# Expert 7's weights in a permanent place and loaded first, both static blocks in rounded halves within the last queries, half of the weights loaded there

## The chip, the cores and the metric

The kernel runs on one core of a Trainium2 chip. The metric is device time in microseconds (us) of one execution, lower is better. Engines: TensorE (PE; PEld is its weight load), VectorE (DVE), ScalarE (ACT), GpSimd (POOL) and SyncE (SP, which here issues loads and does index arithmetic). SBUF is the on-chip memory, PSUM the small memory that TensorE writes into.

## What is computed

Agent attention, and on its output a routed mixture of experts. B = 4 batches, N = 11456 rows, C = 128; 49 agents; 8 experts with F = 1024.

```
a2k = softmax(agents @ k.T);  agent_v = a2k @ v
x   = softmax(q @ agents.T) @ agent_v              # 45824 rows in all
use = x @ w_skip > 0                               # the others are returned as they are
e   = argmax(x @ w_gate);  g = softmax(x @ w_gate)[e]
out = x + g * (relu(x @ w1[e]) @ w2[e])            # for the rows in use
```

## The kernel before

**Attention** (`attention`, lines 167 to 944). Each batch is cut into 15 chunks of 6 columns of 128 rows, 60 chunks in all. One loop over 79 slots writes out the instructions of all engines in a fixed order (`manual_schedule`): within a slot the words of `ORDER[phase]` (lines 46 to 51) are gone through, and each engine executes its own instructions in the order in which they were written. A slot's number below is counted from the first query slot, as in the variable `at`. Keys, values and queries of different batches overlap ("w"); from slot 46 on only queries of batch 3 are left ("q"). There a slot n does, in this order:

- "qN": `query_norm` of chunk n-4 on VectorE (L479 reciprocal, L487 twice), which frees the only `ps_x` buffer; "qD": `query_weight`, every second slot (L526, L527 on VectorE, L530 on POOL)
- "sQ": `scores` of chunk n-1 on TensorE (L355); "qS": its maximum on VectorE (L444); "qE": six exponentials on ACT (L450)
- "qG": the gate's maximum on VectorE (L516), subtraction on POOL (L517), exponential on ACT (L518), every second slot
- "qT": transposes on TensorE (L458) and a copy on ACT (L460); "qO": the output DMA, on ACT's queue
- "rt", "rx": a step of the router (`codes`, `ranks`, `routing`; mostly VectorE, some POOL)
- "mX": `query_mix` of chunk n-3 on TensorE (L471), which needs `ps_x`; "sb", "sa": `static` before and after it
- "wt": one conversion of weights, if due (below)

**Loads.** `prefetch` (lines 820 to 835) goes through a list of loads in the order of the slots that need them, up to eight slots ahead, and stops where no buffer is free. There are 13 buffers (`many`): 8 tiles `ld` (`few`) and 5 in the region `lds`. SP issues the loads, each after the last reader of its buffer.

**Weights.** An expert's weights come in four tiles of 256 KB. `weights` (line 332) rounds a tile to the high half on ACT (L340, fp32r) and subtracts on POOL for the low half (L341). Experts 0 to 5 have a permanent place, `w`, and start every 1.95 slots from slot 2 on. Expert 7's halves lie in `late`, over the ring of scores, and start at slots 47 to 50; expert 6's lie in `shared`, over `lds`, at slots 61 to 64. Expert 7's float32 tiles stay in their buffers (`st["whole"]`) for the static blocks.

**Static blocks.** The first two blocks of 384 rows of expert 7 are known once batch 0 is routed. They are computed within attention, in float32: `layer1` (line 746, L749), ReLU on ACT (L750), `layer2` (line 752, L756), two steps behind. `STATIC` says how many items of the list are done by which slot: block 0 in slots 50 to 60, block 1 from slot 61 on into the last `routing`, which calls `static` four times. `sums` (L761) copies a block's sum on ACT. `early_rows` brings the rows, and `early_x` (line 787: L790 on ACT, L791 on VectorE, at slot 64) the rows of the first dynamic block.

**Dynamic blocks** (`experts`, lines 947 to 1409). 37 blocks of 384 rows, one expert after the other, 7 first. `block` (line 1374) does 48 products of rounded operands (three per tile: high x high, low x high, high x low; L1363, L1369), transposes (L1357, L1351) and the index products (L1344); the low half of the hidden layer is L1190 on VectorE. Expert 7 has a loop of its own (lines 1402 to 1404); `passed` (line 986) then branches (L989) to the code of the others, with a hint that `block` put into TensorE's stream (`mark_branch_hint_location`). Its own code is aligned at its end (line 992).

## Time and profile before

| what | us |
|---|---|
| median of three runs | 709.5 |
| lowest, highest | 707.9, 710.36 |
| the profiled execution | 710.59 |
| its span, first to last instruction | 708.8 |

The page gives busy time over the span: TensorE 633.8 us (89%), its weight load 583.6, VectorE 519.8, ACT 370.0, POOL 359.6. Of the span's slices the DMA row is at 8 or 9 tenths for the first 15 of 40 (about 266 us) and at 1 in the second half. Matmul ends are modelled, so a busy TensorE is not one at its peak. In the timeline each row has start, length, engine, line, operation, output<-input, count, and in brackets how long the engine had been idle before it and what ended that. A float32 product is two records (x2), a rounded one is one.

### The profile page before, as it was taken

To read this page: it belongs to the slowest core of one execution; us is meant where nothing else is said; L and a number is where in the kernel's file an instruction comes from. 1 tells how busy PE (TensorE), PEld (TensorE's weight loads), DVE (VectorE), ACT (ScalarE), POOL (GpSimd) and SP (SyncE) were. 2 spreads that over 40 slices of the span, in tenths; PEclk is the share of its full clock that TensorE was granted. 3 is DMA by queue.
4 is the path that set the end of the run, shared out by engine and by line. 5 is a ranking of instruction groups with operands and counts; after the bars stand their busy time and mean duration, and the time that the engine had idled before them with its cause. 6 is when DMAs were issued, how large, how long until landed. Compare 5 with 4: busy or idle time off the path is not lost. (4 is left out here: it accounts for less than half of the span.)

```text
span 708.8 us, 20720 instructions
## 1 busy us (share of the span) xinstructions
PE 633.8 (89%) x6776; PEld 583.6 (82%) x6776; DVE 519.8 (73%) x1797; ACT 370.0 (52%) x1036; POOL 359.6 (51%) x457
## 2 busy tenths in 40 slices
PE   5689789878897879995799799999999999999995
PEld 5589678767786767673589799999999999999995
DVE  4226657887878777766678588888888888888784
ACT  3346466546454655554255355555555555555552
POOL 2322352256335463303476456666666666666653
PEclk9799899989978995999799899999999999999998
DMA  8999899999999896443022111111111111111100
GB/s 315 356 365 324 284 365 397 385 337 349 396 353 332 283 359 236 159 153 140 24 56 50 38 31 41 41 45 41 45 41 45 45 45 41 42 43 46 42 30 9
DMA packets 59677, 119.20 MB, mean 168 GB/s; under 512 B 14982, under 2 KB 23306, under 8 KB 59600
## 3 DMA queue, kind: packets, MB, share of 16 engines
q1 hardware_dynamic: 43184, 79.92, 32.5%
q10 hardware_dynamic: 8928, 23.79, 8.5%
q0 software_dynamic: 7488, 14.54, 7.2%
q8 instruction: 40, 0.66, 0.4%
q14 instruction: 37, 0.30, 0.1%
HBM read 87.18 MB, written 31.50 MB: 167 GB/s over the span
## 5 line engine op out<-in xcount | busy, mean ns | idle before, releaser
L1255 ACT ACTIVATE hh<-h 128x384 fp32r<-128x384 f32 x296 | 145.1, 491 | 98.2 <-ACTq L974 94.0
L1190 DVE SCALAR_TENSOR_TENSOR hl<-h,hh 128x384 fp32r<-128x384 f32 x296 | 155.9, 553 | 35.2 <-DVEq L974 31.4
L1281 POOL DMA_INDIRECT xg<-out_dram,ids x108 | 110.0, 1018 | 84.7 <-issue 74.3
L1295 POOL DMA_INDIRECT out_dram<-xo,sid x117 | 116.9, 999 | 46.0 <-issue 33.8
L1369 PE MATMUL y<-hh,w 128*128 128x384 f32 x512 | 136.7, 348 | 0.1
L1363 PE MATMUL h<-xh,w 128*128 128x384 f32 x512 | 132.4, 340 | 3.9 <-PEq L974 3.9
L450 ACT ACTIVATE qe<-ps_s,qm 128x49 f32<-128x49 f32 x360 | 75.4, 313 | 42.3 <-DVE qm L444 35.0
L1363 PEld LDWEIGHTS h<-xh,w 128*128 128x128 f32 x512 | 93.8, 190 | 4.5 <-issue 4.5
L1369 PEld LDWEIGHTS y<-hh,w 128*128 128x128 f32 x512 | 89.1, 189 | 0.2 <-issue 0.2
L1363 PE MATMUL h<-xl,w 128*128 128x384 f32 x256 | 87.1, 340 | 0.0
L1369 PE MATMUL y<-hl,w 128*128 128x384 f32 x256 | 86.3, 337 | 0.0
L355 PE MATMUL ps_s<-agT,ld 128*64 128x49 f32 x1728 | 67.2, 237 | 15.2 <-DMA ld<-in_k_dram 6.2
L355 PEld LDWEIGHTS ps_s<-agT,ld 128*64 128x64 f32 x1728 | 62.6, 152 | 20.8 <-issue 12.2
L471 PE MATMUL ps_x<-av,eT 50*128 50x138 f32 x720 | 65.1, 318 | 2.4 <-DVE G L487 2.3
L471 PEld LDWEIGHTS ps_x<-av,eT 50*128 50x128 f32 x720 | 51.9, 206 | 14.1 <-issue 10.5
L487 DVE TENSOR_TENSOR xs<-ps_x,qr 128x768 f32<-128x768 f32 x60 | 57.5, 959 | 5.6 <-DMA out_dram<-xs 2.2
L444 DVE TENSOR_REDUCE qm<-ps_s 128x6 f32<-128x294 f32 x60 | 27.4, 457 | 40.4 <-PE ps_s L355 38.3
L395 POOL TENSOR_TENSOR scores<-scores,mb 128x294 f32<-128x294 f32 x60 | 44.7, 771 | 24.0 <-DVE mb L390 24.0
L355 PEld LDWEIGHTS ps_s<-agT,lds 128*64 128x64 f32 x1152 | 41.7, 150 | 10.0 <-issue 3.2
L355 PE MATMUL ps_s<-agT,lds 128*64 128x49 f32 x1152 | 45.7, 236 | 3.8 <-ACT qe L450 2.0
L1363 PEld LDWEIGHTS h<-xl,w 128*128 128x128 f32 x256 | 48.8, 190 | 0.0
L1251 ACT ACTIVATE yT<-y 128x384 f32<-128x384 f32 x37 | 18.1, 490 | 58.6 <-ACTq L974 58.6
(199 smaller groups left out, 1078.8 us busy)
## 6 DMA issues: line engine op xcount, KB each, us to landing
out_dram<-xs ACTq DMA_DIRECT2D x60, 387.0 KB, 6.4
ld<-in_v_dram SPq DMA_DIRECT2D x37, 387.0 KB, 6.7
ld<-in_k_dram SPq DMA_DIRECT2D x37, 384.0 KB, 7.0
ld<-in_q_dram SPq DMA_DIRECT2D x35, 384.0 KB, 6.3
lds<-in_q_dram SPq DMA_DIRECT2D x25, 384.0 KB, 6.0
lds<-in_v_dram SPq DMA_DIRECT2D x23, 387.0 KB, 7.5
lds<-in_k_dram SPq DMA_DIRECT2D x23, 384.0 KB, 7.5
ld<-in_moe_w_dram SPq DMA_DIRECT2D x23, 256.0 KB, 5.8
```

Of the source, the lines that this page charges most:

```text
L355: r.append(ten.matmul(pt[h : h + 64, t * NA : (t + 1) * NA], lhsT=xT[:, t * P + h : t * P + h + 64], rhs=agT[:, b, :], start=True, stop=True))
L395: pool.tensor_tensor(out=x, in0=x, in1=st["mb", chunks[n][0]].unsqueeze(1).to_broadcast(x.shape), op=ALU.subtract)
L444: vec.tensor_reduce(st["qm", n], st["qs", n], axis=AX.X, op=ALU.max, negate=True)
L450: act.activation(qes[n % PAR["qe"]][:, t, :NA], s[:, t, :], AF.Exp, bias=mx[:, t : t + 1])
L471: ten.matmul(px[:, h, t, :], lhsT=eT[s, t * P : (t + 1) * P], rhs=st["av", b][s, :], start=True, stop=True)
L487: vec.tensor_tensor(out=out[:r, h, j, :], in0=px[:r, h, j, w], op=ALU.mult, in1=rs[:r, h, j].unsqueeze(3).to_broadcast(list(px[:r, h, j, w ...
L1190: v.scalar_tensor_tensor(out=hl[:, f], in0=h_ps[f % HB], scalar=0.0, in1=hh[:, f], op0=ALU.max, op1=ALU.subtract).then_inc(sem["HL"], 1)
L1255: s.activation(hh[:, f], h_ps[f % HB], AF.Relu).then_inc(sem["HH"], 1)
L1281: g.indirect_dma_start(out=xg[n % TURN][:, h, :], out_offset=None, in_=out, in_offset=bass.IndirectOffsetOnAxis(ap=ids[:, n % TURN, h : h ...
L1295: g.indirect_dma_start(out=out, out_offset=bass.IndirectOffsetOnAxis(ap=sid[:, n % 2, h : h + 1], axis=0), in_=xo[:, n % 2, h, :], in_offs ...
L1363: w = t.matmul(h_ps[f % HB], lhsT=ps.w1[e][wx][:, cs], rhs=x, start=(n == 0), stop=(n == 2))
L1369: w = t.matmul(y_ps, lhsT=ps.w2[e][wx][:, f, :], rhs=h[:, f], start=(f == 0 and n == 0), stop=(f == FC - 1 and n == 2))
```

## The change

1. Places: the list of places is reordered, so that expert 5 gets `shared`, expert 6 `late`, and expert 7 the sixth part of `w`.
2. Order of the weights: 7, 0, 1, 2 every 2.7 slots from slot 2 to 42; 3, 4, 5, 6 every 0.9 slots from slot 46 to 59. No float32 tile stays behind.
3. Buffers: 5 `ld`, 3 `more`, 5 `lds`. From slot 41 on loads take `ld` only. The hidden halves of the static blocks, `hs`, lie over `more`.
4. Static blocks: three rounded products for each float32 one. `layer1` writes the high half on ACT and the low half on VectorE; `layer2` reads both. `rows` makes a high half on ACT and a low half on VectorE of the rows of blocks 0 and 1 and of the first dynamic block. All 38 items stand in slots 48 to 61, after "mX"; `routing` calls `static` no more.
5. `key_shift` of batch 0 (L395): every second chunk on VectorE in place of POOL.
6. The loop of expert 7's blocks is aligned to 256 instructions on TensorE.

```diff
-PAR = dict(cols=6, ld=8, more=5, qe=3, eT=2, xs=5, tail=3, first=3, ahead=2, h=4,
-           weights=(12, 195, 100), late=(-13, 1))
-STATIC = {("sa", i - 10): 2 + i * 16 // 10 for i in range(11)}
-STATIC.update({("sb", 1): 18, ("sb", 2): 20, ("sa", 2): 25})
+PAR = dict(cols=6, ld=5, more=5, qe=3, eT=2, xs=5, tail=3, first=3, ahead=2, h=3, few=-6,
+           weights=((2, 270), (46, 90)))
+STATIC = {("sa", i): 38 + (i - 1) * 37 // 13 for i in range(-12, 2)}
...
-        parts += [[x[:, i * F : (i + 1) * F] for i in range(4)] for x in (self.shared, late)]
+        parts[-1:-1] = [[x[:, i * F : (i + 1) * F] for i in range(4)] for x in (self.shared, late)]
...
+        size = PAR["h"] * PAR["cols"] * (C + 1)
+        self.more = a("more", [P, -(-size // 32) * 32], F32).ap()[:, :size]
+        self.hs = nc.alloc_sbuf_tensor_at("hs", [P, PAR["h"], 2, TB], F32R, offset=nc.sbuf_base - -(-size // 32) * 128).ap()
...
-        many = few + [ps.lds[:, i * LD : (i + 1) * LD] for i in range(PAR["more"])]
+        rooms = [ps.more[:, i * LD : (i + 1) * LD] for i in range(PAR["h"])]
+        many = few + rooms + [ps.lds[:, i * LD : (i + 1) * LD] for i in range(PAR["more"])]
...
-            pool.tensor_tensor(out=x, in0=x, in1=st["mb", chunks[n][0]].unsqueeze(1).to_broadcast(x.shape),
+            eng = vec if n < NCH and n % 2 else pool
+            eng.tensor_tensor(out=x, in0=x, in1=st["mb", chunks[n][0]].unsqueeze(1).to_broadcast(x.shape),
...
-                static(28)
...
-                static(31)
...
-                static(len(items))
...
+        def rows(x):
+            pt = turned_rows((x - 1) % TURN)
+            behind(act.copy(ps.xh, pt), st["last"])
+            behind(vec.tensor_tensor(out=ps.xl, in0=pt, in1=ps.xh, op=ALU.subtract), st["last"])
+            if x == AHEAD_STATIC:
+                behind(pool.tensor_copy(ps.db, ps.drow[:, 0, :].unsqueeze(1).to_broadcast([P, 2 * NB, sh.NC + 1])), st["last"])
...
+        def layer1(f):
+            pt = ps_s.tile([P, 512], F32, name="ps_s")[:, :TB]
+            for n, (w, x) in enumerate(((0, ps.xh), (1, ps.xh), (0, ps.xl))):
+                ten.matmul(pt, lhsT=ps.w1[NE - 1][w][:, f * P : (f + 1) * P], rhs=x, start=(n == 0), stop=(n == 2))
+            i = f % PAR["h"]
...
+            hi, lo = (ps.hs[:, i, x, :] for x in range(2))
+            before = reads.get(id(rooms[i]), [])
+            behind(act.activation(hi, pt, AF.Relu), before)
+            behind(vec.scalar_tensor_tensor(out=lo, in0=pt, scalar=0.0, in1=hi, op0=ALU.max, op1=ALU.subtract), before)
...
+        def layer2(f):
             if f == 0:
+                st["y"] = ps_a.tile([P, 512], F32, name="ps_a")[:, :TB]
+            for n, (w, h) in enumerate(((0, 0), (1, 0), (0, 1))):
+                ten.matmul(st["y"], lhsT=ps.w2[NE - 1][w][:, f, :], rhs=ps.hs[:, f % PAR["h"], h, :],
+                           start=(f == 0 and n == 0), stop=(f == FC - 1 and n == 2))
...
         for x in range(2):
+            items.append((rows, x))
+            for f in range(FC + PAR["ahead"]):
+                items += [(layer1, f)] * (f < FC) + [(layer2, f - PAR["ahead"])] * (f >= PAR["ahead"])
             items.append((sums, x))
             if x == 0:
                 items.append((first_result,))
+            else:
+                items.insert(-1, (rows, AHEAD_STATIC))
...
-        early_w = [(e, i) for e in range(NE - LATE) for i in range(4)]
...
+        for (at, step_), es in zip(PAR["weights"], ((NE - 1, 0, 1, 2), (3, 4, 5, 6))):
+            for j, n in enumerate((e, i) for e in es for i in range(4)):
+                starts.setdefault(sh.Q0 + at + j * step_ // 100, []).append(n)
...
-                bufs = few if kind == "w" and n[0] >= NE - LATE else many
+                bufs = many if i < late + PAR["few"] else few
...
-                if at == n_all + 4:
-                    early_x()
...
+            t.addr_align(256, offset=0, max_nops=0)
             with t.While(ps.left[0]):
                 hint = block(NE - 1, t.mark_branch_hint_location)
```

## Rows read from the trace of the kernel before

**Rows 1.** Busy time by stretch: stretch length, engines' busy us, granted clock, DMA share, GB/s.
```profile
30.00:40.00 10.00, 10.00 (x140) 9.91 (x140) 0.00 (x0) 6.28 (x14) 9.29 (x13) 0.75 0.88 289
100.00:200.00 100.00, 85.95 (x1597) 75.49 (x1595) 76.61 (x239) 54.47 (x204) 39.52 (x67) 0.93 1.01 375
260.00:284.00 24.00, 21.74 (x185) 17.19 (x184) 17.81 (x64) 13.78 (x52) 9.44 (x15) 0.58 0.75 261
284.00:322.00 38.00, 35.47 (x444) 25.16 (x444) 27.48 (x79) 22.45 (x87) 7.53 (x20) 1.00 0.44 151
```

**Rows 2.** Timeline, POOL, the key shifts of batch 0.
```profile
28.49 10.80 POOL L395 TENSOR_TENSOR scores<-scores,mb 128x294 f32<-128x294 f32 x15 [24.00 <-DVE mb L390]
```

**Rows 3.** Lines L374 and L1190: ns least/median/most, first and last start.
```profile
L374 DVE TENSOR_TENSOR run<-scores,run x56: 400/466/1139, 9.5 to 220.3; 128x294 f32<-128x294 f32 x56
...
L1190 DVE SCALAR_TENSOR_TENSOR hl<-h,hh x296: 543/554/559, 350.5 to 698.6; 128x384 fp32r<-128x384 f32 x148
```

**Rows 4.** DMA issues, KB each, median us to landing: 275 to 300 us, then all.
```profile
lds<-in_q_dram SPq DMA_DIRECT2D x3, 384.0 KB, 3.1
...
ld<-in_v_dram SPq DMA_DIRECT2D x37, 387.0 KB, 6.7
```

**Rows 5.** Timeline, PE, two products of the static block 1.
```profile
329.17 0.81 PE L756 MATMUL ps_a<-ld,ld 128*128 128x384 f32 x2
329.81 0.81 PE L749 MATMUL ps_s<-run,ld 128*128 128x384 f32 x2
```

**Rows 6.** Timeline, one query slot with a static product, 303.9 to 307.4 us.
```profile
303.98 0.46 DVE L444 TENSOR_REDUCE qm<-ps_s 128x6 f32<-128x294 f32 x1 [0.96 <-PE ps_s L355]
304.34 0.98 PE L471 MATMUL ps_x<-av,eT 50*128 50x138 f32 x12
...
304.48 1.26 ACT L450 ACTIVATE qe<-ps_s,qm 128x49 f32<-128x49 f32 x6 [1.50 <-DVE qm L444]
...
305.37 0.20 DVE L479 RECIPROCAL qr<-ps_x 128x6 f32<-128x6 f32 x1
...
305.77 0.51 ACT L460 COPY eT<-ps_e 128x384 f32<-128x384 f32 x1
...
306.20 0.49 ACT L750 ACTIVATE ld<-ps_s 128x384 f32<-128x384 f32 x1
...
306.53 0.20 DVE L487 TENSOR_TENSOR G<-ps_x,qr 128x54 f32<-128x54 f32 x1
...
306.94 0.23 DVE L527 RECIPROCAL gs<-gs 128x12 f32<-128x12 f32 x1
```

**Rows 7.** Timeline, DVE, L479 of slots 48 and 61 (of 60, one per chunk).
```profile
269.11 0.20 DVE L479 RECIPROCAL qr<-ps_x 128x6 f32<-128x6 f32 x1 [0.30 <-PE ps_x L471]
...
319.23 0.20 DVE L479 RECIPROCAL qr<-ps_x 128x6 f32<-128x6 f32 x1 [0.76 <-PE ps_x L471]
```

**Rows 8.** Timeline, the end of attention.
```profile
328.68 0.14 DVE L516 TENSOR_REDUCE top<-G 128x6 f32<-128x48 f32 x1
...
330.17 1.26 POOL L341 TENSOR_TENSOR shared<-ld,shared 128x512 fp32r<-128x512 f32 x1 [4.76 <-ACT shared L340]
...
333.84 0.56 DVE L791 TENSOR_TENSOR xl<-ps_s,xh 128x384 fp32r<-128x384 f32 x1 [4.26 <-ACT xh L790]
...
343.87 0.16 DVE L670 SCALAR_TENSOR_TENSOR rec<-ps_e,every 128x8 f32<-128x8 f32 x1
345.58 0.48 ACT L761 COPY yT<-ps_a 128x384 f32<-128x384 f32 x1 [2.09 <-PE ps_a L756]
```

**Rows 9.** Line L989, the branches behind expert 7, of SP's and TensorE's queues: ns.
```profile
L989 SPq COMPARE_BRANCH  x1: 45/45/45, 365.9 to 365.9; - x1
L989 PEldq COMPARE_BRANCH  x1: 3184/3184/3184, 397.6 to 397.6; - x1
```

**Rows 10.** Timeline, PE, the transpose L1357 of four blocks, one per block.
```profile
390.40 0.49 PE L1357 MATMUL yt<-ident,yT 128*128 128x128 f32 x3
...
405.21 0.41 PE L1357 MATMUL yt<-ident,yT 128*128 128x128 f32 x1
...
415.35 0.49 PE L1357 MATMUL yt<-ident,yT 128*128 128x128 f32 x3
...
424.57 0.27 PE L1357 MATMUL yt<-ident,yT 128*128 128x128 f32 x1
```

## The prediction

> **What bounds the kernel now.** I read the stretches first [rows 1]. From 100 to 200 us the DMA engines are busy all the time (share 1.01) and TensorE is not. [...] From 284 to 322, the last queries, DMA is at 0.44 and the clock is full: no bandwidth limit there, but a chain of short operations per slot. Behind that comes the router's chain on VectorE [rows 8], and then the blocks, on TensorE without gaps but for one, behind expert 7 [rows 9, 10]. So a saving counts if it is DMA traffic before 260 us, a link of the slot chain in the last queries, a link of the router's chain, or that gap. The profiled execution took 710.59 us, 1.8 more than its span and 1.1 over the median of 709.5; the sum is made on 710.59, and 1.1 is taken off at the end.

> **Key shifts of batch 0 (L395).** Fifteen run on POOL back to back, 10.80 us, 0.72 each [rows 2]. Seven go to VectorE, where the nearest form (L374, same tile) takes 0.47 at the median and up to 1.14 [rows 3]. If both engines worked freely, the eight left would end 5.0 us earlier. What that can return is the DMA time lost meanwhile: share 0.88 over 30 to 40 us against 1.01 later [rows 1], 1.3 us. I take -0.5, as L374's spread shows that it is held up at times; ends 0 and -1.3. [...]

> **Weights later.** Counting the starts by hand, 23 tiles of 256 KB are due before query slot 45 now and 16 then: 7 fewer. At 375 GB/s [rows 1] one takes 0.70 us, 7 take 4.9. That holds while DMA is full, and by 260 us it is no longer. I take -3.0; ends 0 and -4.9. The tiles moved to slots 46 to 59 meet a DMA share of 0.44: nothing there.

> **Five load buffers from slot 41 on.** Walking the load loop by hand, in these slots every load is now issued two or more slots ahead of its use. After the change value chunks 56 and 58 take a buffer that the scores of queries 42 and 43 free one slot earlier, and TensorE has only a mix (L471, 0.98 us [rows 6]), a transpose and one value chunk in between, about 2 us. A load lands in 3.1 us in a quiet stretch and in 6.7 at the median [rows 4]. Each of the two waits is then 1 to 4.7 us. I take +2.5 for both, near the quiet end; ends 0 and +9.

> **The static blocks in halves.** On TensorE they get cheaper: a float32 product (two records) starts 0.64 us after the one before it [rows 5], 32 of them take 20.5 us. The steady loop does 48 rounded products and nine small ones in 9.22 us [rows 10], at most 0.19 each; 96 take 18.2. That is not the bound. The bound is the order on VectorE. After the change each first-layer step issues two evictions: the high half on ACT, then the low half on VectorE, which needs the high half. Both stand at the end of a slot (after "mX", as "sa"). So on VectorE the low half stands **ahead of the next slot's L479**, and on ACT the high half stands behind that slot's six exponentials (L450) and copy (L460), which need L444, which is behind L479. That closes a ring through both engines that is open now, since the ReLU feeds only TensorE. [Rows 6] show one slot: L479 starts at 305.37 although the ReLU (L750) ends only at 306.69. With the low half ahead of it, L479 would start at 306.69 + 0.1 + 0.55 = 307.34, 2.0 us later; 0.55 is L1190, the same operation [rows 3]. One crossing of this kind exists now: L791 kept VectorE idle for 4.26 us until ACT came to L790 [rows 8].

> The ring: from L479 to the end of L527 1.80, but only to the end of L487, 1.36, in every second slot: 1.6; from L444 to the end of the ReLU 306.69 - 303.98 = 2.7; a hand-over and the low half 0.65. Together 4.95 us a slot. By the new STATIC table VectorE gets 18 such writes in 12 slots (48 to 53 and 55 to 60; slot 54 has none). 12 x 4.95 = 59.4; six writes beyond the first of a slot, 0.55 each, 3.3; slot 54 as now, 3.5; the lead that VectorE has over ACT is lost once, 2.0; the first result in slot 55, a transpose and a copy, 1.0. Sum 69.2 us from the L479 of slot 48 to that of slot 61. Now these 13 slots take 319.23 - 269.11 = 50.1 [rows 7]. So +19.1; slot 61, with the third split of rows, adds about 1. **I take +20.** [...]

> The eight more conversions in these slots (POOL 1.26 each [rows 8], half of that on ACT) fall into the idle part of the ring; without the ring ACT, now busy 22.45 of 38 us [rows 1], still has room for 5 more.

> **The end of attention.** Expert 6's conversions leave the router's chain. Now POOL works on L341 until 331.43, and VectorE waits for L791 and goes on with the router at 334.40, although L516, on which the next step rests, was done at 328.82 [rows 8]. Without the conversions that step needs two short operations on POOL and ACT, about 1.2 us. That is -4.3, and the chain to L670 behind it stays. L670 ends at 344.03, but ACT's copy of the second static block at 346.06 [rows 8], and only then can the blocks begin; the copy moves to slot 61, another -2.0. I take -6.3; ends -2 and -7.

> **Aligned loop of expert 7.** The branch behind it (L989) took TensorE's queue 3184 ns, SP's branch of the same line 45 ns [rows 9]; both have a hint ahead. From transpose to transpose that block took 405.21 - 390.40 = 14.81 us and the next 10.14, against 9.22 in the steady loop [rows 10]: 6.5 us in all. If the branch becomes like SP's, -6.0, with half a microsecond left over; if not, 0. I take -6.0, at three in four. [...]

> **Sum.** -0.5 - 3.0 + 2.5 + 20 - 6.3 - 6.0 = +6.7: 717.3 on the profiled execution, **716.2 us** on the median.

> **The rivals.**
> 1. *The branch still misses* (the alignment doesn't do what it is there for). For: the hint is there now and fails. Against: SP's 45 ns. 716.2 + 6.0 = 722.2.
> 2. *Faster: VectorE's idle time swallows the low halves.* Place: the last queries, where VectorE is busy 27.48 of 38 us [rows 1]; 18 x 0.55 = 9.9 us fit into the 10.5 idle. [...] It decides where the 13 slots grow by less than 1.0 us each, since the other terms sum to -13.3. For: the shares. Against: the order of the queues, as told, and L791's 4.26 us.
> 3. *The loads starve.* With five buffers the two waits cost 9 and not 2.5: 722.7. For: the landings of 6.7 us under load. Against: DMA is at 0.75 by then.

> **How the numbers follow.** Forecast 0.46 (its own range 710 to 721), rival 1 0.17, rival 2 0.27, rival 3 0.10. About 0.3%, 2.1 us, can be told from no change: 707.4 to 711.6 is the same. Rival 2 lies below 707.4 in most of its range (0.24) and the forecast in little of its own (0.01): faster 0.25. Same: 0.03 of rival 2 and 0.10 of the forecast. The rest, 0.62, is slower. From 700 to 723 lie 0.45 of the forecast and 0.13, 0.17 and 0.06 of the rivals: 0.81.

> **What would show it.** In the changed profile L479 should come every 5 us in slots 49 to 61, with ACT's high half as what ended VectorE's idle time before the new low half, and TensorE should wait at L471 for L487. L989 on TensorE's queue should be under 0.4 us, and the block behind it near 9.3. From the end of the last L516 to the end of L670 it should be 11 us, now 15.2. I am wrong if the slots stay under 4.5 us, if the branch takes 3 us again, or if the value chunks of slots 44 and 45 wait more than 3 us each.

## The result, and the profile after

The changed kernel takes 709.95 us, the kernel before in the same rounds 707.13 (medians of 20 runs each): ratio 1.0063 [1.0038, 1.0088], slower by 4.4 us by the ratio (the medians alone differ by 2.8). The fourth set below gave 1.0070 [1.0038, 1.0103]. Slower was forecast (+6.7 us), 716.2 was not: the kernel before came out 2.4 us under the 709.5 on which the sum stood, and the change at two thirds of its size.

In the second and third of the four sets of runs below every traced kernel's blocks took some 12.3 us instead of 9.2, and a run, of the kernel before too, about 820 us (the third set's chip gave 705 later), so that their ratios are compared within a set, and their traces read for the branch and for what comes ahead of the blocks.

Five starts carry the comparison. L479 starts once per slot (chunk n in slot n + 4), so that its starts in slots 4, 44, 48 and 61 (chunks 0, 40, 44 and 57 in the expectations) cut attention in three; then come the last L479 and the first block. All from the timeline, in us:

| kernel | first L479 | slots 4 to 44 | 44 to 48 | 48 to 61 | run against before |
|---|---|---|---|---|---|
| before | 56.94 | 194.17 | 18.00 | 50.12 | |
| changed | 56.81 | 185.18 | 23.20 | 67.61 | 1.0063 |
| changed, fourth set | 56.25 | 187.84 | 23.44 | 70.06 | 1.0070 |

The stretches of the changed kernel, which answer to [rows 1] (length, busy us of TensorE, its weight loads, VectorE, ACT, POOL; granted clock, DMA share, GB/s; the last queries now end at 341 us):
```profile
30.00:40.00 10.00, 10.00 (x143) 9.94 (x142) 4.33 (x5) 5.17 (x14) 5.71 (x7) 0.77 0.87 294
100.00:200.00 100.00, 87.07 (x1689) 77.06 (x1690) 79.39 (x248) 56.29 (x215) 38.92 (x69) 0.95 1.00 372
260.00:284.00 24.00, 18.97 (x209) 15.69 (x209) 17.91 (x62) 13.90 (x48) 10.97 (x13) 0.79 0.68 224
284.00:337.00 53.00, 41.67 (x473) 35.22 (x473) 33.00 (x94) 30.41 (x103) 19.49 (x30) 0.97 0.56 184
```
In the last queries no engine is full: TensorE, the busiest, works 41.67 of 53 us, VectorE 33.00. What VectorE waits for in that stretch, and what TensorE waits for (us in total, times, longest):
```profile
DVE hs L751 <- ACT hs L750: 14.3, 11, 2.6
...
PE ps_x L471 <- DVE G L487: 11.9, 10, 2.0
```
L751 is the new low half, L750 the high half. One slot of the changed kernel, as [rows 6] show one of before:
```profile
307.52 0.45 DVE L444 TENSOR_REDUCE qm<-ps_s 128x6 f32<-128x294 f32 x1
...
307.75 1.75 PE L471 MATMUL ps_x<-av,eT 50*128 50x138 f32 x12 [1.95 <-DVE G L487]
...
308.01 1.26 ACT L450 ACTIVATE qe<-ps_s,qm 128x49 f32<-128x49 f32 x6 [1.23 <-DVE qm L444]
...
309.43 1.01 PE L745 MATMUL ps_s<-xh,w 128*128 128x384 f32 x2
...
310.79 0.49 ACT L750 ACTIVATE hs<-ps_s 128x384 fp32r<-128x384 f32 x1 [0.85 <-PE ps_s L745]
...
311.31 0.56 DVE L751 SCALAR_TENSOR_TENSOR hs<-ps_s,hs 128x384 fp32r<-128x384 f32 x1 [1.88 <-ACT hs L750]
...
312.08 1.08 DVE L751 SCALAR_TENSOR_TENSOR hs<-ps_s,hs 128x384 fp32r<-128x384 f32 x2 [0.21 <-ACT hs L750]
...
313.09 0.18 DVE L479 RECIPROCAL qr<-ps_x 128x6 f32<-128x6 f32 x1
...
314.59 0.97 PE L471 MATMUL ps_x<-av,eT 50*128 50x138 f32 x12 [1.22 <-DVE G L487]
```
The circle (the prediction's ring) can be read off it: the mix (L471), behind it TensorE's static product (L745), ACT's high half, 1.88 us of idle VectorE, the low half, and only then the L479 and L487 for which TensorE's next mix has waited 1.22 us.

What answers to [rows 8]: the router's last steps, then TensorE's first block.
```profile
342.87 0.14 DVE L516 TENSOR_REDUCE top<-G 128x6 f32<-128x48 f32 x1
...
352.76 0.16 DVE L667 SCALAR_TENSOR_TENSOR rec<-ps_e,every 128x8 f32<-128x8 f32 x1
...
355.14 0.98 PE L1347 MATMUL h<-xh,w 128*128 128x384 f32 x2 [2.67 <-PEq L958]
```
The branch behind expert 7, of [rows 9], is now L973 (ns), and the transposes of [rows 10] are L1341:
```profile
L973 SPq COMPARE_BRANCH  x1: 45/45/45, 373.1 to 373.1; - x1
L973 PEldq COMPARE_BRANCH  x1: 370/370/370, 404.7 to 404.7; - x1
```
```profile
397.65 0.49 PE L1341 MATMUL yt<-ident,yT 128*128 128x128 f32 x3
...
407.61 0.49 PE L1341 MATMUL yt<-ident,yT 128*128 128x128 f32 x3
```
The block with the branch takes 9.96 us (14.81 before), the next 9.20.

### The profile page after: what moved, and what is told of

Same layout as the page of the kernel before. It is cut to its first block, busy times and chain, and to the rows that moved or that the text cites. A ratio compares the mean times of both kernels' runs of the same rounds, so it can differ in the third digit from the quotient of the medians.

```text
span 709.9 us, 20810 instructions
## 1 busy us (share of the span) xinstructions
PE 621.0 (87%) x6808; PEld 582.7 (82%) x6808; DVE 529.5 (75%) x1822; ACT 368.8 (52%) x1036; POOL 356.4 (50%) x450
## 5 line engine op out<-in xcount | busy, mean ns | idle before, releaser
L1353 PE MATMUL y<-hh,w 128*128 128x384 f32 x592 | 157.1, 346 | 1.3 <-PEq L958 1.2
L1347 PE MATMUL h<-xh,w 128*128 128x384 f32 x592 | 153.2, 340 | 3.6 <-PEq L958 3.5
L1347 PEld LDWEIGHTS h<-xh,w 128*128 128x128 f32 x592 | 107.4, 190 | 8.8 <-issue 8.7
L1353 PEld LDWEIGHTS y<-hh,w 128*128 128x128 f32 x592 | 102.5, 188 | 1.6 <-issue 1.6
L450 ACT ACTIVATE qe<-ps_s,qm 128x49 f32<-128x49 f32 x360 | 75.4, 311 | 52.6 <-DVE qm L444 45.4
L1347 PE MATMUL h<-xl,w 128*128 128x384 f32 x296 | 100.6, 340 | 0.0
L1353 PE MATMUL y<-hl,w 128*128 128x384 f32 x296 | 99.0, 335 | 0.0
L471 PE MATMUL ps_x<-av,eT 50*128 50x138 f32 x720 | 64.2, 314 | 19.0 <-DVE G L487 18.3
L471 PEld LDWEIGHTS ps_x<-av,eT 50*128 50x128 f32 x720 | 51.7, 203 | 30.7 <-issue 23.9
L354 PE MATMUL ps_s<-agT,ld 128*64 128x49 f32 x1320 | 53.3, 238 | 11.7 <-DMA ld<-in_k_dram 6.1
L354 PEld LDWEIGHTS ps_s<-agT,ld 128*64 128x64 f32 x1320 | 49.1, 153 | 17.2 <-issue 13.2
L487 DVE TENSOR_TENSOR xs<-ps_x,qr 128x768 f32<-128x768 f32 x60 | 57.5, 959 | 3.9 <-DVE qr L479 0.5
L1353 PEld LDWEIGHTS y<-hl,w 128*128 128x128 f32 x296 | 55.6, 188 | 0.0
L395 POOL TENSOR_TENSOR scores<-scores,mb 128x294 f32<-128x294 f32 x53 | 41.1, 801 | 23.8 <-DVE mb L389 23.8
L444 DVE TENSOR_REDUCE qm<-ps_s 128x6 f32<-128x294 f32 x60 | 26.8, 446 | 32.1 <-PE ps_s L354 30.0
L1235 ACT ACTIVATE yT<-y 128x384 f32<-128x384 f32 x37 | 18.2, 491 | 58.1 <-ACTq L958 58.1
L354 PE MATMUL ps_s<-agT,lds 128*64 128x49 f32 x1008 | 37.5, 228 | 5.9 <-ACT qe L450 4.7
```

The lines of the kernel that those rows point to most:

```text
L354: r.append(ten.matmul(pt[h : h + 64, t * NA : (t + 1) * NA], lhsT=xT[:, t * P + h : t * P + h + 64], rhs=agT[:, b, :], start=True, stop=True))
L395: eng.tensor_tensor(out=x, in0=x, in1=st["mb", chunks[n][0]].unsqueeze(1).to_broadcast(x.shape), op=ALU.subtract)
L444: vec.tensor_reduce(st["qm", n], st["qs", n], axis=AX.X, op=ALU.max, negate=True)
L450: act.activation(qes[n % PAR["qe"]][:, t, :NA], s[:, t, :], AF.Exp, bias=mx[:, t : t + 1])
L471: ten.matmul(px[:, h, t, :], lhsT=eT[s, t * P : (t + 1) * P], rhs=st["av", b][s, :], start=True, stop=True)
L487: vec.tensor_tensor(out=out[:r, h, j, :], in0=px[:r, h, j, w], op=ALU.mult, in1=rs[:r, h, j].unsqueeze(3).to_broadcast(list(px[:r, h, j, w ...
```

## The experiments

**1. Without the directive** (first set, as 2 to 4).
```diff
-            t.addr_align(256, offset=0, max_nops=0)
```

> The changed kernel without the one alignment directive ahead of expert 7's loop; everything else is the change. Theory (the directive alone cures the first return of the loop): TensorE's branch goes from 370 ns back to about 3.2 us, the block behind it from 9.96 us back to some 14.8, and the run is 5 to 6.7 us slower than the changed kernel, about 1.5% above the kernel before. Rival A (the shorter loop cured itself, because the static blocks moved elsewhere and the code lies otherwise now): the branch stays under 0.5 us and the time does not move. Rival B (the branch comes back but the blocks of SyncE or POOL wait anyway): branch 3 us, the time 0 to 2 us slower.

Ratio 1.0069 [1.0033, 1.0105], as with it, and the branch keeps its 369 ns:
```profile
L973 PEldq COMPARE_BRANCH  x1: 369/369/369, 408.5 to 408.5; - x1
```
The theory fell, rival A held. In the changed kernel the directive does nothing that the runs can tell; something else had cured the branch.

**2. The low halves one slot later.** L751 is put on a list and issued in the next slot behind "qN qD", ahead of "sQ".
```diff
-    "q": "qN+4 qD+5 sQ+1 qS+1 ...
+    "q": "qN+4 qD+5 lo sQ+1 qS+1 ...
```

> The changed kernel with one thing moved: VectorE's low half of a static layer is issued one query slot later, right after that slot's first query work, instead of right behind the high half of its own slot; the same instructions, the same number of them. Theory (the ring: within a slot VectorE waits in order for ACT's high half, ACT for TensorE's product, TensorE for what VectorE gives): the slots from chunk 44 to 57 go from 5.2 us (67.6 us for 13) back to 3.9 to 4.2, and the run is 12 to 15 us faster than the changed kernel, some 697 us. Rival A (VectorE is simply loaded: the low halves and the key shifts fill it): the same work in another order gives under 3 us. Rival B (the loads cannot follow at 3.9 us a slot, so the wait passes to the value and query loads): about half, 5 to 8 us, and waits on DMA appear in the slots from 50 on.

Ratio 0.9893 [0.9853, 0.9933], 699.34 us: 1.7 points below the changed kernel, 12 us. Slots 48 to 61 take 53.90 us in place of 67.61, with the same instructions. The waits in the last queries, 284 to 326 us:
```profile
ACT qe L450 <- DVE qm L444: 6.2, 9, 1.2
...
PE ps_s L354 <- DMA ld<-in_q_dram: 1.8, 1, 1.8
```
The two waits of the circle are down to 0.3 us (L471 on L487) and 0.9 us (the low half, now L779, on ACT), where the changed kernel had 11.9 and 14.3. Over the same 268 to 322 us in both kernels they are
```profile
PE ps_x L471 <- DVE G L487: 2.3, 2, 1.9
...
DVE hs L779 <- ACT hs L750: 0.9, 3, 0.4
```
against 8.8 and 13.3 us in the changed kernel. The order on VectorE is shown to be the cause: a cause in its load would have stayed, since the instructions are the same. Some 3.8 us over the 50.12 of the kernel before are left.

**3. More load buffers until three slots later.**
```diff
-PAR = dict(..., few=-6,
+PAR = dict(..., few=-3,
```

> The changed kernel with the three buffers of the later hidden halves given to loads until three slots later (few=-3 for -6); nothing else. Theory (the value chunks of slots 41 to 43 came late because only five buffers were left when they were issued, which cost 5.2 us between chunk 40 and 44): TensorE's two waits on value loads of 1.98 and 1.02 us go, the stretch from chunk 40 to 44 shrinks by about 5 us, and the run is 4 to 5 us faster. Rival (the ring sets the end of the queries whatever comes earlier, or the loads are bound by the traffic of expert weights and not by buffers): the stretch does not shrink, or what it gains is lost by chunk 57; under 1 us.

Ratio 1.0013 [0.9983, 1.0042], 3.5 us under the changed kernel (4 to 5 expected). Slots 44 to 48 take 19.61 us (23.20), the other two stretches 187.72 and 67.90. In the changed kernel these two waits stood at the value chunks, and here none:
```profile
250.91 0.87 PE L412 MATMUL ps_a<-ld,scores 128*49 128x129 f32 x12 [1.98 <-DMA ld<-in_v_dram]
...
252.80 1.26 PE L412 MATMUL ps_a<-ld,scores 128*49 128x129 f32 x12 [1.02 <-DMA ld<-in_v_dram]
```
The ring did not swallow the gain, nor give any.

**4. The kernel before with the directive.**
```diff
+            t.addr_align(256, offset=0, max_nops=0)
             with t.While(ps.left[0]):
```

> The kernel before with only the alignment directive ahead of expert 7's loop. Theory: the first return costs TensorE 0.37 us instead of 3.18 and the block behind it 9.96 us instead of 14.8; the run is 5 to 6.7 us faster than before, ratio near 0.991. Rival (the code's place before the loop decides, and in the kernel before 256-byte alignment is not what was missing): no change within 0.3%.

Ratio 0.9927 [0.9890, 0.9963], 5.2 us faster. The branch takes 370 ns, the block 10.04 us, the next 9.24:
```profile
386.30 0.49 PE L1357 MATMUL yt<-ident,yT 128*128 128x128 f32 x3
...
396.34 0.49 PE L1357 MATMUL yt<-ident,yT 128*128 128x128 f32 x3
...
405.58 0.49 PE L1357 MATMUL yt<-ident,yT 128*128 128x128 f32 x3
```
So there the directive is worth all of the term, and in the changed kernel nothing (1). Attention's code is that of before, and its slots 4 to 44 took 190.89 us: 3.3 less than in the profiled execution of before.

**5. Weights early again** (second set).
```diff
-           weights=((2, 270), (46, 90)))
+           weights=((2, 195), (53, 90)))
-... ((NE - 1, 0, 1, 2), (3, 4, 5, 6)) ...
+... ((NE - 1, 0, 1, 2, 3, 4), (5, 6)) ...
```

> The changed kernel with one part undone: five experts' weights (7, 0, 1, 2, 3) and expert 4's again come from the second query slot at one chunk of weights in 1.95 slots, as before, and only 5 and 6 in the last slots. Theory (loading half the weights later takes traffic from the first 40 slots): chunk 0 to 40 takes 3 to 6 us longer than the 185.2 to 188.9 us of the four kernels that load late, of which about 1 us comes back in the slots from 40 to 44 where fewer weights arrive; the run is 2 to 5 us slower than the changed kernel. Rival A (these slots are not bound by traffic, and the shorter stretch was an execution's luck): under 1 us. Rival B (what is loaded early frees the last slots more than it costs before): faster by 2 us or more.

Ratio 1.0194 [1.0141, 1.0246]; the stretches 193.62, 22.33 and 67.76. What the late loading gives between slots 4 and 44 is there, and 1 to 2 us of it come back from 44 to 48. The run is 1.2 points, some 9 us, above 7 of the same set, which is as the changed kernel: more than the 2 to 5 of the theory, and 14 does not repeat it.

**6. Both mends at once** (2 and 3).

> The changed kernel with the low halves issued one slot later and the three hidden-half buffers given to loads until three slots later, both at once. Theory (two causes in two stretches, chunk 40 to 44 and chunk 44 to 57, which add): 12 us from the first and 3.5 from the second as each measured alone, so some 15 us faster than the changed kernel, about 694.5 us, ratio near 0.984. Rival (with the ring open the loads are what the last slots wait for, and they take back what the buffers give): no better than the low halves alone, 699 us.

Ratio 0.9969 [0.9926, 1.0011]; 184.43, 19.54 and 60.19. The rival was nearer, the two stretches didn't add: TensorE now waited 2.36 us at 293.36 for a query chunk, and slots 48 to 61 took 6 us more than in 2.

**7. All key shifts on POOL.**
```diff
-            eng = vec if n < NCH and n % 2 else pool
+            eng = pool
```

> The changed kernel with one part undone: all key shifts on POOL again. Theory (the 16 key chunks wait for their loads, not for POOL): the first query result comes at the same time as in the changed kernel, 55.2 to 56.9 us, and the run does not move, within 1 us. Rival (VectorE's half of the shifts was worth up to 1.3 us): the first query result 0.5 to 1.3 us later, and so the run.

Ratio 1.0076 [1.0036, 1.0115], as the changed kernel within the intervals, which are too wide to tell 1 us; the first L479 comes at 54.59 us, sooner if anything. Line L395 of the changed kernel (ns least/median/most) and its timeline:
```profile
L395 POOL TENSOR_TENSOR scores<-scores,mb x8: 774/997/1003, 28.2 to 34.9; 128x294 f32<-128x294 f32 x8
L395 DVE TENSOR_TENSOR scores<-scores,mb x7: 467/1035/1039, 28.1 to 33.3; 128x294 f32<-128x294 f32 x7
```
```profile
28.12 6.21 DVE L395 TENSOR_TENSOR scores<-scores,mb 128x294 f32<-128x294 f32 x7
28.24 7.46 POOL L395 TENSOR_TENSOR scores<-scores,mb 128x294 f32<-128x294 f32 x8 [23.75 <-DVE mb L389]
```

**8. The high half on VectorE too.**
```diff
-            behind(act.activation(hi, pt, AF.Relu), before)
+            behind(vec.tensor_scalar(hi, pt, 0.0, None, op0=ALU.max), before)
```

> The changed kernel with the high half of a static layer made by VectorE too, in the place where VectorE made only the low half: it has 12 more instructions of some 0.6 us in the slots, but no longer waits for ACT within a slot. Theory (the crossing to ACT and back is the ring's dear link): VectorE's 13.3 us of waits for the high half go and some 7 us of work come, so the slots from chunk 44 to 57 fall from 67.6 to about 61 to 64 us, the run 3 to 6 us faster. Rival (VectorE's load in the slot sets their length, whatever it waits for): 7 us more, 74 us for these slots and the run 5 to 7 us slower.

Ratio 1.0098 [1.0065, 1.0132]; slots 48 to 61 take 69.00 us, between the theory's 61 to 64 and the rival's 74. The waits from 284 to 339 us:
```profile
PE ps_x L471 <- DVE G L487: 12.1, 10, 2.1
...
DVE hs L750 <- PE ps_s L745: 7.8, 7, 1.6
```
The wait for ACT is gone, half of it stays as a wait for TensorE's product, the rest became work (VectorE 41.36 of 55 us), and the wait that closes the circle is the old one. The crossing to ACT was not the dear link; with 2, the reading is that it is dear that VectorE's queue waits within the slot for a product that stands behind the mix.

**9. and 10. The loop's directive with an offset of 64 and of 128** (third set, one execution each). The list of the change counts the directive's numbers in instructions; where an expectation says bytes, the same numbers are meant.
```diff
-            t.addr_align(256, offset=0, max_nops=0)
+            t.addr_align(256, offset=64, max_nops=0)
```

> The changed kernel with expert 7's loop put 64 bytes past a 256-byte line instead of on it; nothing else. Theory (the place of the loop's code decides the first return, and the change without the directive happened to lie well): TensorE's branch is 3.2 us and the block behind it 14.8 us, as in the kernel before, some 5.7 us more. Rival (the place does not matter, and the kernel before missed for what its other static blocks and loops left behind): 0.37 us and 10 us as in the changed kernel with and without the directive.

> The same with 128 bytes past the line. Theory: a slow first return at one of the two places at least (3.2 us against 0.37 us). Rival: 0.37 us here too; then the place is not what decides.

Line L973, at 64 and at 128:
```profile
L973 PEldq COMPARE_BRANCH  x1: 367/367/367, 430.8 to 430.8; - x1
```
```profile
L973 PEldq COMPARE_BRANCH  x1: 3452/3452/3452, 428.7 to 428.7; - x1
```
The offset decides, with the same code: at 0 the branch takes 0.37 us (370 ns in the changed kernel), at 64 0.37 too, at 128 3.45 (192 wasn't tried), so that the theory for 64 missed and that for 128 held. What runs beside the slow branch is in the trace too, a packet of 16 KB (0.02 MB in the view; the page of the kernel before has 40 of them in 0.66 MB) of the kind "instruction" on the DMA queue q8. In the kernel before one starts at 398.16 us, 0.6 us after the branch, and takes 1.07 us (the branch's window is 397.55 to 400.74 us); at 128 one lies in the branch's window too (428.65 to 432.11):
```profile
q8 instruction: 1, 0.02, 2.1%
```
```profile
q8 instruction: 1, 0.02, 2.5%
```
In the changed kernel the branch takes 0.37 us at 404.7 us, and no such packet starts between 368.65 and 405.76 us. In ten further runs (1, 3 to 9, 11 and 12) the branch takes 0.36 to 0.38 us. So both slow branches have such a packet in them, and the changed kernel's fast one has none; that a slow branch waits for the packet is inferred from this and not measured. So is that the changed kernel's loop lies at a good place without the directive (1), and the kernel before's at a bad one.

**11. and 12. Both mends again, and with the last weights spread.** 12 is 6 with one number changed.
```diff
-           weights=((2, 270), (46, 90)))
+           weights=((2, 270), (46, 105)))
```

> The low halves one slot later and three more load buffers until three slots later, once more, on another chip than the first time, where all kernels' blocks ran at 12.3 us instead of 9.2. Theory (two causes that add): ratio to the kernel before near 0.984. Rival (as the first trace showed: chunk 40 to 44 gains 4 us, but the slots from 50 on wait for query loads and give back 6 of it): no better than the low halves alone, 0.989.

> The same two edits, and the last four experts' weights spread over 15.75 slots (one chunk in 1.05 slots, for 0.9), which takes 14% of their traffic from the slots 46 to 61. Theory (with the ring open the query loads share the ring of transfers with the weights): the two waits on query loads of some 2.5 us in slots 50 to 52 shrink, 1 to 3 us faster than with weights in 14.4 slots. Rival (buffers, not traffic, make these loads late): no change within 1 us, or slower because the last weights come after the last query.

11: ratio 0.9926 [0.9888, 0.9964]; 191.01, 15.79, 58.13. 12: 0.9897 [0.9833, 0.9961]; 184.20, 19.03, 56.18. The intervals overlap; the last stretch shrinks by 2 to 4 us, and TensorE's wait for query loads in it, 2.1 us in 11 and 2.4 in 6, is 1.0 in 12. Traffic and buffers are not told apart by this: weights that come later also hold fewer buffers.

**13. to 15. On one chip, in the same rounds: the changed kernel, weights early, all three mends.**

> The changed kernel itself, as the base of the two beside it. Theory: chunk 0 to 40 in 184 to 189 us, 40 to 44 in 22.5 to 26, 44 to 57 in 67 to 70; some 0.6% over the kernel before. Rival (the small loss was an accident of the first measurement's runs): no difference to before.

> The changed kernel with weights loaded early, beside the changed kernel in the same rounds. Theory (the term is -6.6 us and was mis-sized at -3.0): 6 to 9 us slower than the changed kernel, chunk 0 to 40 in 190 to 194 us. Rival (the term is -3.0 as forecast, and the rest is what executions differ by): 2 to 4 us slower, chunk 0 to 40 in 187 to 190 us.

> Low halves one slot later, three more load buffers until three slots later, the last weights spread over 15.75 slots, beside the changed kernel in the same rounds. Theory (ring, buffers and traffic are three causes that add): 14 to 17 us faster than the changed kernel, 1.3 to 1.7% under the kernel before. Rival (only the ring counts): 12 us faster than the changed kernel, 1.1% under the kernel before.

| kernel | median | against before (705.41) | slots 4 to 44 | 44 to 48 | 48 to 61 |
|---|---|---|---|---|---|
| changed | 710.77 | 1.0070 [1.0038, 1.0103] | 187.84 | 23.44 | 70.06 |
| weights early | 715.53 | 1.0109 [1.0064, 1.0155] | 193.45 | 22.13 | 66.65 |
| all three mends | 696.33 | **0.9837 [0.9797, 0.9877]** | 185.22 | 20.69 | 55.74 |

The first came as expected. The second has the stretch of its theory (193.45) and a time in between: 4.8 us over the changed kernel by the medians, 2.8 by the ratios. The last beats both kernels, as its theory had it: by the medians 9 us under the one before and 14 under the changed, by the ratios 11.5 and 16. Its L479 of slots 48 and 61 (changed kernel of the first profile: 265.19 and 332.80):
```profile
260.78 0.20 DVE L479 RECIPROCAL qr<-ps_x 128x6 f32<-128x6 f32 x1
```
```profile
316.52 0.20 DVE L479 RECIPROCAL qr<-ps_x 128x6 f32<-128x6 f32 x1 [0.76 <-PE ps_x L471]
```

## Why the prediction was right in direction and wrong in size

The measured 709.95 us lies just under the 710 at which the forecast's own range begins, 6.3 under 716.2. The step that failed first is the base on which the sum was made: it holds 2.4 us of the 6.3. The sum was too high as well: +6.7, where the two sets say 2.7 to 6.2 and 2.7 to 7.3 us. In it two terms were mis-sized, with errors that cancel: weights later, -3.0, measured -6.5 in its stretch, and five load buffers, +2.5, measured +6.1 in theirs. The loop's -6.0 came, but not by the directive to which it was put down.

**The base**: "The profiled execution took 710.59 us, ... 1.1 over the median of 709.5". That median stood on three runs. The 20 runs of before beside the changed kernel have a median of 707.13 and go from 700.32 to 710.36, so the profiled execution is above all of them; the one of 4, with the same code in attention, took 3.3 us less in slots 4 to 44 alone. A row is one draw, and so was the base.

**Key shifts** (-0.5): nothing that 7 shows; within its ends. The engines held each other up, as L374's spread had said: 1.03 us for VectorE's shift, whose first took 0.47, and 1.00 for POOL's, which alone takes 0.77 (median of the kernel before). The last shift ends at 35.70 in place of 39.29 us, 3.6 sooner and not the 5.0 of working freely. The 3.6 us bought nothing to be seen: the DMA share from 30 to 40 us stayed (0.88, 0.87).

**Weights later** (-3.0, at most -4.9): the first place where a term was mis-sized. The four kernels that load early take 190.9 to 194.2 us for slots 4 to 44, mean 193.0; the 13 that load late 184.2 to 191.0, mean 186.5. That is -6.5, outside the ends, but not all of it is weights. By the start of slot 44 the kernel before had issued 24 tiles of weights, 60 value and 47 query loads, the changed kernel 16, 58 and 45: the tiles are fewer about as counted, and four chunk loads of some 385 KB had also slipped past the cut, as the five buffers hold them back (with 3 it is 60 and 46). So the next slots belong to it: slots 4 to 48 take 210.7 us with the changed load order (mean of eight executions) and 215.8 with weights early (5 and 14), -5.1, and 1.3 of it come back in slots 48 to 61, -3.8 in all. By the runs, 0.39 points between 13 and 14, it is about 2.8 us, near the forecast, with intervals of 0.3 and 0.5 points; by 5 and 7 it was 9. The size of the whole stays open.

**Five load buffers** (+2.5, from 0 to +9): the second. Slots 44 to 48 go from 18.0 to 24.1 us, +6.1 (24.1 is the mean of the eight, from 22.85 to 26.01); about 2 of it go with the late weights, as 22.2 with weights early shows, about 4 with the buffers, as 3 gives back (3.5 us of the run). TensorE's two waits were 1.98 and 1.02 us, as priced; what I had not counted is the queue behind them: VectorE waits 4.6 us for the value chunk that came late (L420 on L412), and from chunk 41 to 42 it takes 9.30 us where the kernel before took 4.35. Rival 3 put +9 on it. By stretch the errors of these two terms are -3.5 and +3.6 and cancel, in part because the same loads moved over the cut at slot 44: over slots 4 to 48 the two were forecast at -0.5 and came to +0.2 (210.7 against 210.5, the mean of the kernel before and 4).

**The static blocks in halves** (+20): right, in mechanism and nearly in size. From slot 48 to 61 I forecast 69.2 us; 66.7 to 70.1 came. The circle is there with both of its waits, and goes when the order is opened (2). One link was misjudged, the turn through ACT: without it the slots are no shorter (8). Rival 2, that idle time swallows the low halves, fails: VectorE was idle for 20 of 53 us, and yet the 13 slots grew by 1.35 us each, where rival 2 needed less than 1.0.

**The end of attention** (-6.3): L516's end to L667's end is 352.92 - 343.01 = 9.9 us (11 forecast, 15.2 before). From the last L479 to the first block 355.14 - 341.12 = 14.02 us, 20.79 before: -6.8.

**The aligned loop** (-6.0): 9.96 for 14.81 us in the block, 9.20 for 10.14 in the next: -5.8, as large as forecast, but not by the directive. In the kernel before it would have given 5.2 us by itself (4); the changed kernel had them without it (1), and an offset of 128 alone brings the slow branch back, 3.45 us (10). I had the branch's price from the row, and no row for its cause: that the alignment would bear on it was my assumption. Both slow branches, 3.18 and 3.45 us, have a 16 KB packet of the kind "instruction" in them, and the changed kernel's of 0.37 us has none. Why the branch is slow with the offset of 128 no run here shows.

**The sum** by these stretches: 0 + 0.2 (slots 4 to 48) + 18.4 (mean of six executions with the ring and the changed load order, 68.5 us) + 0.6 (slots 61 to 63) - 6.8 - 5.8 = +6.6, against 4.4 to 4.9 measured by the runs, with upper ends of 6.2 and 7.3. Where the two microseconds between lie no run shows; one trace a kernel, with stretches that differ by more than that, can't tell.

## What to carry to other kernels

Where engines run a written order, price an added instruction by what stands behind it in its queue: 18 writes of 0.55 us came with 17.5 us more in a stretch where VectorE had been idle for a quarter of the time, and issuing 16 of them one slot later, past the work that the next turn of the loop waits for, gave back 13.7. A branch that is slow once may be a matter of the code's place (here 0.37 us at offsets 0 and 64, 3.45 at 128), so another edit can seem to have cured it (3.18 us before, 0.37 in 1 without the directive): try the place alone before crediting the edit. And before a forecast of under 1%, weigh the profiled execution against many runs, since its stretches can lie 3 us off, or more: slots 4 to 44 took 184.43 us in 6 and 191.01 in 11, the same kernel. And where an edit holds loads back, don't book two stretches apart if the loads only move from one to the other.
